# One core, attention and two mixing layers in one kernel: the first attention by head pairs, the second one later, small transfers on another queue, weight decoding spread evenly

## The chip, the core and the metric

The kernel runs on one core of a Trainium2 chip. The core has five engines that run their own instruction lists in order and meet only at semaphores: TensorE (PE in the profile, its weight loads as PEld) multiplies matrices, VectorE (DVE) and ScalarE (ACT) do elementwise work, GpSimd (POOL) sets memory here, and SyncE (SP) issues transfers. Any of SP, ACT and POOL can issue a transfer; it then stands in that engine's own list. The metric is the time of the whole program on the device, in microseconds. Half a per cent of it is 3.8 us.

## What is computed

Eight batches of 8 heads, 576 tokens and 64 channels a head. Three steps follow one another; the output is float32.

```python
kv = einsum('bhsd,bhse->bhde', k, v);  out = einsum('bhsd,bhde->bhse', q, kv)
x  = out / sqrt(mean(out*out, -1) + 1e-6) * g_norm          # linear attention, then (b, s, 512)
gate = sigmoid(sum_k conv_w[k] * x shifted by k)            # causal convolution, 5 taps
x  = gate * (x @ w_val) @ w_out
theta = x @ w_theta;  zr, zi = x*cos(theta), x*sin(theta)
u  = x + w_tok_r @ zr + w_tok_i @ zi                        # mixes tokens
out = u + relu(u @ w_ch)
```

The weights arrive as 64-bit floats. The kernel turns them into float32 by bit operations ("decoding"), and keeps each of them, and each operand of a large product, as a high part and a low part, so that one product is three matmuls.

## The kernel before

Channels lie on the 128 partitions as four blocks (`NM = 4`), tokens run along the free dimension in two halves of 288. The program has a start, a loop over the batches i = 0 to 7, and a last phase.

**Attention of one batch.** `load_kv` and `load_q` (lines 151 to 169) load keys and values (`kv`, four tiles, one for each pair of heads) and queries (`q`, two tiles) on SP's queue; a GpSimd memset goes ahead of each `kv` tile. `key_value` (171) multiplies keys by values into one PSUM tile `kvp`, which ACT copies to `kvs`. `attention` (187) is a generator in three pieces. The first two make a half of the tokens each: for both groups of pairs, 8 matmuls into `o`, the squares `sq` on ACT (204), and `x` = `o` times the norm's gain on ACT (205). The third piece sums the squares on PE (`ss`, 212), and DVE takes 1/sqrt in 12 small operations (219 to 225, the result is `y`, 128x72). For b >= 2 (`SPREAD`) `y` then goes to DRAM as `rd` and comes back spread over the partitions as `yb` (228 to 233), by transfers on SP's queue; for b = 0 and 1 PE spreads it by small matmuls.

**Normalizing.** `normalize` (237) multiplies `x` by `yb` on DVE (246 or 257) in two halves, and splits each into `xh` (ACT) and `xl` (DVE, line 69).

**First product and gate.** `conv` (261) makes the gate `acc` of one channel block: one multiplication on ACT, four multiply-adds on DVE (265), the sigmoid on ACT. `value` (278) makes for each block m 24 matmuls `v`, then DVE multiplies the gate by them (288) and the result is split into `gh` and `gl`. `first` (294) multiplies by `w_out` into `y` (lines 274 to 276 again), ACT copies to `yo`, SP stores it to DRAM as `yd`. In the trace the name `y` on PE is this product, and `y` on DVE is the 1/sqrt.

**The loop.** Batch i runs `value(i)`, and between its blocks `key_value(i+2)` (at m = 1, followed by the loads of `kv` for i+3) and the two halves of `attention(i+2)`; then `normalize(i+1)`, `first(i)` with the third piece of `attention(i+2)` in it, and the first two gates of i+1. Behind that stands the decoding of later weights: chunks `wt` of w_theta (`todo`) and `tk` of the token matrices (`toks`), each some four DVE passes of 128x512 (94 to 98); a decoded `tk` goes back to DRAM as `td`. `RATE = (1, 3)` asks for one `wt` and three `tk` in a batch, and batch 6 takes all that is left. These chunks have the lowest priority: the scheduler places them wherever the order of the program leaves an engine free by its own reckoning. `issue_after(x)` keeps what is under it behind x.

**The start.** `START` (31) is the order of the loads on SP's queue (v: chunks of w_val, o: of w_out, k: key and value tiles, q: queries, c: the taps and the gain; 0 to 3 belong to batch 0, 4 to 7 to batch 1). Then come `key_value(0)`, three chunks of w_val, the taps, `attention(0)`, `normalize(0)`, `key_value(1)`, `attention(1)`, the first gates, and the last chunk of w_val.

**Around i = 7.** The attention's memory is given back, `load_y(0)` loads the result of batch 0 (`f`) on SP's queue, DVE transposes it (`fT`, 321), it goes through DRAM (`sd`, `yt`), two chunks of w_ch are fetched on POOL's queue and decoded. Behind batch 7 the last phase begins: `theta` (`tht`, `th`), sines, and the token matrices `tok` read back from `td` and split into `wkh` and `wkl`, with which the products `u` start. From there on PE has the work of eight batches before it.

Of the kernel before, what the change touches and what calls it, by code (L numbers as in the profile page):

```python
# [8 lines left out]
F32 = mybir.dt.float32  # L9
# [21 lines left out]
START = "v0 k0 k1 v1 k2 k3 v2 q0 q1 q2 q3 c0 v3 o0 k4 k5 k6 k7 o1 q4 q5 q6 q7 o2 o3"  # L31
WVFIRST = 3
SPREAD = 2
EARLY = 2
RATE = (1, 3)
# [8 lines left out]
def attention_moe_holo_kernel(ctx, tc, kvm, kvt, qt, gn, w_val, conv_w, w_out, w_th, w_tok, w_ch, outT):  # L44
# [126 lines left out]
    def key_value(b, kv):  # L171

        ps = one_bank(f"kvp{b}")
        for g in range(2):
# [9 lines left out]
        kvs_of[b] = pa.tile([P, NP, D], F32, tag="kvs", bufs=2, name=f"kvs{b}")  # L184
        nc.scalar.activation(kvs_of[b], ps[:, 0:NP * D].rearrange("p (a e) -> p a e", e=D), AF.Copy)

    def attention(b, q):

        kv = kvs_of.pop(b)
# [3 lines left out]
        for h in range(2):  # L193
            sl = slice(h * HS, (h + 1) * HS)
            for g in range(2):
                o = two_banks(f"o{b}_{h}_{g}")
                for e in range(2):
                    for j in range(2):
                        rows = slice(j * D, (j + 1) * D)
                        mm = nc.tensor.matmul(o[e * D:(e + 1) * D, j, :], kv[rows, 2 * g + e, :], q[g][rows, e, sl],  # L200
                                              start=True, stop=True, tile_position=(j * D, e * D))
                ch = slice(2 * g, 2 * g + 2)
                sq[h, g] = px.tile([P, 2, HS], F32, tag="sq", bufs=4, name=f"sq{b}_{h}_{g}")
                nc.scalar.activation(sq[h, g], o, AF.Square, scale=0.125)
                nc.scalar.activation(x[:, ch, PAD + h * HS:PAD + (h + 1) * HS], o, AF.Copy, scale=gsb)
            yield x
# [19 lines left out]
        if b >= SPREAD:  # L226

            nc.sync.dma_start(out=rdram[b], in_=y)
            yb = px.tile([P, NM, S], F32, tag="yb", bufs=1, name=f"yb{b}")
            src = rdram[b].rearrange("(k r) x -> k (r x)", k=NM)  # L230
            for i in range(2):
                rows = src[:, i * S:(i + 1) * S].unsqueeze(0).to_broadcast([D, NM, S])
                nc.sync.dma_start(out=yb[i * D:(i + 1) * D], in_=rows)
# [35 lines left out]
    def product(ps, w, m, xh, xl, t0, chunks=range(4)):  # L269
        tsl = slice(t0, t0 + HS)  # L270
        wh, wl = w
        for k in chunks:
# [3 lines left out]
            nc.tensor.matmul(ps, wh[:, m, ks], xl[:, k, tsl], start=False, stop=(k == 3))  # L276

    def value(b, x, xh, xl, sg, between):
        gh = pa.tile([P, NM, S], F32R, tag="gh", bufs=1, name=f"gh{b}")
        gl = pa.tile([P, NM, S], F32R, tag="gl", bufs=1, name=f"gl{b}")  # L280
        for m in range(NM):
            between(m)
            g = sg[m]
            ps = two_banks(f"v{b}_{m}")
            for h in range(2):
                product(ps[:, h], wv, m, xh, xl, h * HS)
# [323 lines left out]
```

## Time and profile before

| | us |
|---|---|
| median of 3 runs | 752.65 (750.66 to 753.38) |
| the profiled execution | 753.31 |
| its span, first to last instruction | 751.5 |
| outside the span | 1.8 |
| PE busy | 709.7 |
| DVE busy | 523.9 |
| ACT busy | 335.9 |
| POOL busy | 20.7 |
| mean granted TensorE clock, share of full speed | 0.986 |

The profile is of one execution. The view of busy time by stretches gives for each stretch its length, then for each engine the busy time and the count of instructions, then the granted TensorE clock, the busy share of the transfer engines and GB/s. The views of waits name the waiting instruction, what it waited for, the total, how often, and the longest. In the timeline a row has the start, the busy time, the engine and line, the operation with its output and inputs, and in brackets the idle time before it with what ended it. A busy time of a group of "x2" or more runs from the first start to the last end.

### The profile page before, as it was taken

The numbers are of one execution on the slowest core, as the hardware profiler recorded it, in microseconds if no ns is written. First come the engines' busy times: TensorE is split into PE (matmuls) and PEld (weight loads), VectorE is DVE, ScalarE is ACT, GpSimd is POOL, SyncE is SP. The second block draws the span as 40 slices with busy tenths as digits, with TensorE's granted clock in tenths as the row PEclk, the third lists the DMA queues.
The fourth block names the chain that finished last, engine by engine and source line by source line (L and its number), as shares of the span: only waits on it lengthen the run. The fifth ranks groups of instructions, "written<-read, shape, count | busy, mean of one in ns | idle before, by whom it ended". The sixth has DMA issues, their size and how long they took to land.

```text
span 751.5 us, 14674 instructions
## 1 busy us (share of the span) xinstructions
PE 709.7 (94%) x6000; PEld 669.9 (89%) x6000; DVE 523.9 (70%) x930; ACT 335.9 (45%) x560; POOL 20.7 (3%) x72
## 2 busy tenths in 40 slices
PE   1679999999989999889999999999999999999998
PEld 1568999798987999879899899999999998998998
DVE  6389969798879999588983872853853835836504
ACT  2366565637464645376541640621622514514301
POOL 4000000000000000000000000000000000000000
PEclk9779999999999999999999999999999999999999
DMA  9948794979896358534345034163051270160101
GB/s 256 285 140 243 209 229 141 229 228 237 219 238 189 108 136 246 190 102 122 111 138 157 9 119 113 32 174 90 17 164 59 69 179 35 64 175 1 64 1 64
DMA packets 77059, 104.88 MB, mean 140 GB/s; under 512 B 11712, under 2 KB 42560, under 8 KB 76992
## 3 DMA queue, kind: packets, MB, share of 16 engines
q1 hardware_dynamic: 76416, 101.85, 48.5%
q0 software_dynamic: 576, 2.10, 0.9%
q8 instruction: 47, 0.77, 0.4%
q14 instruction: 20, 0.16, 0.1%
HBM read 72.73 MB, written 31.19 MB: 138 GB/s over the span
## 4 chain that ended last, share of the span: by engine, by line
PE 60%; DVE 24%; DMA 8%; ACT 4%; issue 3%; SPq 1%; POOL 0%; DVEq 0%; ACTq 0%; POOLq 0%
PE u L513 10%; PE u L511 10%; PE u L512 10%; DVE acc L265 10%; PE c L276 5%; PE c L274 5%; PE c L275 5%; DMA yb<-rd 4%; PE th L459 3%; PE th L457 3%; PE th L458 3%; DMA kv<-in_kvm_dram 2%; DVE x L246 2%; DVE xl L69 2%; DVE acc L288 2%
## 5 line engine op out<-in xcount | busy, mean ns | idle before, releaser
L516 DVE TENSOR_TENSOR f<-u,f 128x288 f32<-128x288 f32 x64 | 26.5, 455 | 129.8 <-PE u L513 129.8
L265 DVE SCALAR_TENSOR_TENSOR acc<-x,cw,acc 128x576 f32<-128x576 f32 x128 | 100.8, 817 | 1.3 <-ACT acc L263 1.3
L68 ACT ACTIVATE uh<-f 128x288 fp32r<-128x288 f32 x64 | 26.2, 444 | 152.4 <-DVE f L516 152.3
L274 PE MATMUL y<-gh,woh 128*128 128x288 f32 x256 | 77.8, 304 | 7.8 <-DVE acc L288 5.4
L274 PE MATMUL v<-xh,wvh 128*128 128x288 f32 x256 | 77.6, 303 | 0.7 <-DVE acc L288 0.7
L276 PE MATMUL v<-xl,wvh 128*128 128x288 f32 x256 | 76.5, 299 | 0.0
L276 PE MATMUL y<-gl,woh 128*128 128x288 f32 x256 | 75.8, 298 | 0.5 <-DVE gl L69 0.5
L275 PE MATMUL y<-gh,wol 128*128 128x288 f32 x256 | 76.0, 297 | 0.0
L275 PE MATMUL v<-xh,wvl 128*128 128x288 f32 x256 | 76.0, 297 | 0.0
L274 PE MATMUL c<-uh,wch 128*128 128x288 f32 x256 | 75.4, 295 | 0.0
L276 PE MATMUL c<-ul,wch 128*128 128x288 f32 x256 | 75.4, 295 | 0.0
L275 PE MATMUL c<-uh,wcl 128*128 128x288 f32 x256 | 75.4, 294 | 0.0
L274 PEld LDWEIGHTS y<-gh,woh 128*128 128x128 f32 x256 | 48.8, 191 | 11.9 <-DVE acc L288 6.1
L274 PEld LDWEIGHTS v<-xh,wvh 128*128 128x128 f32 x256 | 48.7, 190 | 4.6 <-issue 1.7
L459 PE MATMUL th<-wth,yl 128*128 128x512 f32 x128 | 50.3, 393 | 0.0
L458 PE MATMUL th<-wtl,yh 128*128 128x512 f32 x128 | 50.1, 391 | 0.0
L457 PE MATMUL th<-wth,yh 128*128 128x512 f32 x128 | 50.0, 391 | 0.0
L276 PEld LDWEIGHTS y<-gl,woh 128*128 128x128 f32 x256 | 48.4, 190 | 1.2 <-DVE gl L69 1.2
L276 PEld LDWEIGHTS v<-xl,wvh 128*128 128x128 f32 x256 | 48.6, 190 | 0.3 <-issue 0.2
L275 PEld LDWEIGHTS y<-gh,wol 128*128 128x128 f32 x256 | 48.8, 191 | 0.0
L275 PEld LDWEIGHTS v<-xh,wvl 128*128 128x128 f32 x256 | 48.7, 190 | 0.0
L275 PEld LDWEIGHTS c<-uh,wcl 128*128 128x128 f32 x256 | 48.0, 188 | 0.3
(188 smaller groups left out, 1946.0 us busy)
## 6 DMA issues: line engine op xcount, KB each, us to landing
kv<-in_kvm_dram SPq DMA_DIRECT2D x32, 512.0 KB, 8.6
q<-in_qt_dram SPq DMA_DIRECT2D x32, 288.0 KB, 8.9
yd<-yo SPq DMA_DIRECT2D x32, 288.0 KB, 2.4
f<-yd SPq DMA_DIRECT2D x32, 288.0 KB, 3.7
out_dram<-f SPq DMA_DIRECT2D x64, 144.0 KB, 1.8
sd<-fT SPq DMA_DIRECT2D x64, 128.0 KB, 2.5
yt<-sd SPq DMA_DIRECT2D x8, 1024.0 KB, 5.6
yb<-rd SPq DMA_DIRECT2D x12, 576.0 KB, 8.0
```

The source lines that it names most:

```text
L68: one = nc.scalar.activation(h, src, AF.Copy)
L265: nc.vector.scalar_tensor_tensor(a, x[:, m, k:k + S], cw[:, m * 5 + k:m * 5 + k + 1], a, ALU.mult, ALU.add)
L274: nc.tensor.matmul(ps, wh[:, m, ks], xh[:, k, tsl], start=(k == 0), stop=False)
L275: nc.tensor.matmul(ps, wl[:, m, ks], xh[:, k, tsl], start=False, stop=False)
L276: nc.tensor.matmul(ps, wh[:, m, ks], xl[:, k, tsl], start=False, stop=(k == 3))
L457: nc.tensor.matmul(ps, yh[:, k, :], wth[0][:, k, :], start=(k == 0), stop=False)
L458: nc.tensor.matmul(ps, yh[:, k, :], wth[1][:, k, :], start=False, stop=False)
L459: nc.tensor.matmul(ps, yl[:, k, :], wth[0][:, k, :], start=False, stop=(k == 3))
L511: nc.tensor.matmul(ps[:, :HS], zh[:, ms], wkh[:, j, sl], start=(i == 0), stop=False)
L512: nc.tensor.matmul(ps[:, :HS], zh[:, ms], wkl[:, j, sl], start=False, stop=False)
L513: nc.tensor.matmul(ps[:, :HS], zl[:, ms], wkh[:, j, sl], start=False, stop=(i == 8))
L516: nc.vector.tensor_tensor(f[:, m, sl], ps[:, :HS], f[:, m, sl], ALU.add)
```

## The change

- The first attention goes by groups of pairs of heads (both token halves of group 0, then of group 1), its `kvs` is copied group by group, and its `x` is written by DVE (`tensor_scalar`) and no longer by ACT. `START` has the queries of group 0 ahead of the third key tile, one chunk of w_val ahead of all, and the others behind the first batch; the gain is loaded on ACT's queue.
- Only one chunk of w_val is decoded ahead of the first attention, the taps behind it, and the other three chunks between the first gates.
- `key_value(1)` and `attention(1)` move from the start into `value(0)`, and the loads of batch 2 and `key_value(2)`, `attention(2)` behind them.
- `normalize(i+1)` is put behind DVE's `gl` of the last block of `value(i)` (`gs[2]` is the list of the four, `gs[2][-1]` the last), and the decoding of w_out behind that of the second block.
- `rd` and `yb` are issued by GpSimd.
- The third piece of the attention goes 12 matmuls earlier in `first`.
- `RATE` is (1, 2) in every batch from 1 to 6, and batch 6 takes no remainder.

```diff
-START = "v0 k0 k1 v1 k2 k3 v2 q0 q1 q2 q3 c0 v3 o0 k4 k5 k6 k7 o1 q4 q5 q6 q7 o2 o3"
-WVFIRST = 3
+START = "v0 k0 k1 q0 q1 k2 k3 q2 q3 v1 c0 v2 v3 k4 k5 k6 k7 o0 q4 q5 q6 q7 o1 o2 o3"
...
-RATE = (1, 3)
+RATE = (1, 2)
...
     def key_value(b, kv):
...
+        kvs_of[b] = pa.tile([P, NP, D], F32, tag="kvs", bufs=2, name=f"kvs{b}")
...
-        kvs_of[b] = pa.tile([P, NP, D], F32, tag="kvs", bufs=2, name=f"kvs{b}")
-        nc.scalar.activation(kvs_of[b], ps[:, 0:NP * D].rearrange("p (a e) -> p a e", e=D), AF.Copy)
...
-    def attention(b, q):
...
-        kv = kvs_of.pop(b)
+            if b == 0 or g == 1:
+                gs = slice(2 * g if b == 0 else 0, 2 * g + 2)
+                nc.scalar.activation(kvs_of[b][:, gs, :], ps[:, 0:NP * D].rearrange("p (a e) -> p a e", e=D)[:, gs], AF.Copy)
...
+    def attention(b, qs):
...
+        kv, q = kvs_of.pop(b), qs.pop(b)
...
-        for h in range(2):
+        for n in range(4):
...
+            g, h = divmod(n, 2) if b == 0 else (n % 2, n // 2)
...
-            for g in range(2):
-                o = two_banks(f"o{b}_{h}_{g}")
-                for e in range(2):
-                    for j in range(2):
-                        rows = slice(j * D, (j + 1) * D)
-                        mm = nc.tensor.matmul(o[e * D:(e + 1) * D, j, :], kv[rows, 2 * g + e, :], q[g][rows, e, sl],
-                                              start=True, stop=True, tile_position=(j * D, e * D))
-                ch = slice(2 * g, 2 * g + 2)
-                sq[h, g] = px.tile([P, 2, HS], F32, tag="sq", bufs=4, name=f"sq{b}_{h}_{g}")
-                nc.scalar.activation(sq[h, g], o, AF.Square, scale=0.125)
-                nc.scalar.activation(x[:, ch, PAD + h * HS:PAD + (h + 1) * HS], o, AF.Copy, scale=gsb)
-            yield x
+            o = two_banks(f"o{b}_{h}_{g}")
+            for e in range(2):
+                for j in range(2):
+                    rows = slice(j * D, (j + 1) * D)
+                    nc.tensor.matmul(o[e * D:(e + 1) * D, j, :], kv[rows, 2 * g + e, :], q[g][rows, e, sl],
+                                     start=True, stop=True, tile_position=(j * D, e * D))
+            xo = x[:, 2 * g:2 * g + 2, PAD + h * HS:PAD + (h + 1) * HS]
+            sq[h, g] = px.tile([P, 2, HS], F32, tag="sq", bufs=4, name=f"sq{b}_{h}_{g}")
+            nc.scalar.activation(sq[h, g], o, AF.Square, scale=0.125)
+            if b == 0:
+                nc.vector.tensor_scalar(xo, o, gsb, None, ALU.mult)
+            else:
+                nc.scalar.activation(xo, o, AF.Copy, scale=gsb)
+            if n % 2:
+                yield x
...
         sums = one_bank(f"ss{b}")[:, :TB]
...
         if b >= SPREAD:
...
-            nc.sync.dma_start(out=rdram[b], in_=y)
+            nc.gpsimd.dma_start(out=rdram[b], in_=y)
...
-                nc.sync.dma_start(out=yb[i * D:(i + 1) * D], in_=rows)
+                nc.gpsimd.dma_start(out=yb[i * D:(i + 1) * D], in_=rows)
...
-            nc.tensor.matmul(ps, wh[:, m, ks], xl[:, k, tsl], start=False, stop=(k == 3))
+            done = nc.tensor.matmul(ps, wh[:, m, ks], xl[:, k, tsl], start=False, stop=(k == 3))
+        return done
...
     def value(b, x, xh, xl, sg, between):
...
+        lasts, done = [], None
...
-            between(m)
+            between(m, done)
...
-                product(ps[:, h], wv, m, xh, xl, h * HS)
+                done = product(ps[:, h], wv, m, xh, xl, h * HS)
...
-            parts(gh[:, m, :], gl[:, m, :], g)
+            lasts.append(parts(gh[:, m, :], gl[:, m, :], g)[0])
...
-        return gh, gl
+        return gh, gl, lasts
...
     def first(b, gh, gl, between):
...
         part(0, range(3))
         part(1, range(3))
+        between()
...
-        between()
         part(2, range(4))
...
+    nc.scalar.dma_start(out=gsb[0:D], in_=gn)
+    nc.scalar.dma_start(out=gsb[D:P], in_=gn)
...
-            nc.sync.dma_start(out=gsb[0:D], in_=gn)
-            nc.sync.dma_start(out=gsb[D:P], in_=gn)
...
     key_value(0, kvs.pop(0))
-    for k in range(WVFIRST):
-        weight_chunk(px, wv, w_val, k, "wv", raw=raw[f"v{k}"])
+    weight_chunk(px, wv, w_val, 0, "wv", raw=raw["v0"])
+    *_, xy = attention(0, qs)
+    *_, (xs, last) = normalize(0, *xy)
...
-    *_, xy = attention(0, qs.pop(0))
-    *_, (xs, last) = normalize(0, *xy)
-    key_value(1, kvs.pop(1))
-    *_, xy = attention(1, qs.pop(1))
-    sg = [conv(0, m, xs[0]) for m in range(EARLY)]
-    with tc.issue_after(last.ins):
-        for n in range(WVFIRST, 4):
+    sg = []
+    for n in range(1, NM):
+        with tc.issue_after(last.ins):
...
-    kvs[2], qs[2] = load_kv(2), load_q(2)
+        if n <= EARLY:
+            sg.append(conv(0, n - 1, xs[0]))
...
-            ahead = attention(i + 2, qs.pop(i + 2))
...
-        def between(m):
...
-            if two and m == 1:
+            ahead = attention(i + 2, qs)
...
+        def between(m, done):
...
+            if i == 0 and m == 2:
+                with tc.issue_after(done.ins):
+                    key_value(1, kvs.pop(1))
+            if two and i and m == 1:
...
-                next(ahead)
...
+                next(ahead if i else second)
...
+        second = attention(1, qs) if i == 0 else None
...
+        if i == 0:
+            *_, xy = second
+            kvs[2], qs[2] = load_kv(2), load_q(2)
+            key_value(2, kvs.pop(2))
+            kvs[3] = load_kv(3)
+            next(ahead)
...
-            *_, (nxs, last) = normalize(i + 1, *xy)
+            with tc.issue_after(gs[2][-1].ins):
+                *_, (nxs, last) = normalize(i + 1, *xy)
...
-            for k in range(4):
-                weight_chunk(px, wo, w_out, k, "wo", raw=raw[f"o{k}"])
+            with tc.issue_after(gs[2][1].ins):
+                for k in range(4):
+                    weight_chunk(px, wo, w_out, k, "wo", raw=raw[f"o{k}"])
...
-        first(i, *gs, lambda: got.append(next(ahead) if two else None))
+        first(i, *gs[:2], lambda: got.append(next(ahead) if two else None))
...
-                for _ in range(RATE[0] if i < 6 else 8):
+                for _ in range(RATE[0]):
...
-                for _ in range(RATE[1] if i < 6 else 11):
+                for _ in range(RATE[1]):
...
```

The next rows are DVE's list in the program before, at the end of `value(1)`: `x_740` is the `x` of batch 2 and `yb_992` its 1/sqrt, `v_2`, `v_3`, `gl` belong to batch 1.

```order
L288 TENSOR_TENSOR acc_2_1095<-v_2_1196,acc_2_1095 128x576
L69 TENSOR_TENSOR gl_1066<-acc_2_1095,gh_1065 128x576
L246 TENSOR_TENSOR x_740<-x_740,yb_992 128x4x288 x2
L94 TENSOR_SCALAR dst_wt_1481<-raw_wt_1479 128x512
L288 TENSOR_TENSOR acc_3_1189<-v_3_1242,acc_3_1189 128x576
L95 SCALAR_TENSOR_TENSOR dst_wt_1481<-raw_wt_1479,dst_wt_1481 128x512
L69 TENSOR_TENSOR xl_1293<-x_740,xh_1292 128x4x288
L69 TENSOR_TENSOR gl_1066<-acc_3_1189,gh_1065 128x576
L69 TENSOR_TENSOR xl_1293<-x_740,xh_1292 128x4x288
```

The same place in the changed program, where the `x` of batch 2 is `x_769`.

```order
L296 TENSOR_TENSOR acc_2_1096<-v_2_1197,acc_2_1096 128x576
L68 TENSOR_TENSOR gl_1067<-acc_2_1096,gh_1066 128x576
L296 TENSOR_TENSOR acc_3_1190<-v_3_1243,acc_3_1190 128x576
L68 TENSOR_TENSOR gl_1067<-acc_3_1190,gh_1066 128x576
L252 TENSOR_TENSOR x_769<-x_769,yb_975 128x4x288 x2
L93 TENSOR_SCALAR dst_wt_1482<-raw_wt_1480 128x512
L68 TENSOR_TENSOR xl_1294<-x_769,xh_1293 128x4x288 x2
```

The multiplication by `yb` stood ahead of the multiplication by `v_3` and of the last `gl`; it now stands behind both.

DVE's list from the first normalization on, before: `x_282` is the `x` of batch 0, `acc_0` and `acc_1` are its first gates.

```order
L257 TENSOR_TENSOR x_282<-yb_0_0_367,x_282 128x2x288
L257 TENSOR_TENSOR x_282<-yb_0_1_377,x_282 128x2x288
L257 TENSOR_TENSOR x_282<-yb_1_0_389,x_282 128x2x288
L69 TENSOR_TENSOR xl_366<-x_282,xh_365 128x4x288
L257 TENSOR_TENSOR x_282<-yb_1_1_399,x_282 128x2x288
L265 SCALAR_TENSOR_TENSOR acc_0_537<-x_282,cw,acc_0_537 128x576
L265 SCALAR_TENSOR_TENSOR acc_1_544<-x_282,cw,acc_1_544 128x576
L69 TENSOR_TENSOR xl_366<-x_282,xh_365 128x4x288
L265 SCALAR_TENSOR_TENSOR acc_0_537<-x_282,cw,acc_0_537 128x576
L265 SCALAR_TENSOR_TENSOR acc_1_544<-x_282,cw,acc_1_544 128x576
```

And changed, with `x_260` for batch 0; `dst_wv_396` is the second chunk of w_val.

```order
L263 TENSOR_TENSOR x_260<-yb_1_0_367,x_260 128x2x288
L68 TENSOR_TENSOR xl_344<-x_260,xh_343 128x4x288
L263 TENSOR_TENSOR x_260<-yb_1_1_377,x_260 128x2x288
L93 TENSOR_SCALAR dst_wv_396<-raw_wv_170 128x512
L271 SCALAR_TENSOR_TENSOR acc_0_404<-x_260,cw,acc_0_404 128x576
L94 SCALAR_TENSOR_TENSOR dst_wv_396<-raw_wv_170,dst_wv_396 128x512
L68 TENSOR_TENSOR xl_344<-x_260,xh_343 128x4x288
L95 SCALAR_TENSOR_TENSOR dst_wv_396<-raw_wv_170,dst_wv_396 128x512
L271 SCALAR_TENSOR_TENSOR acc_0_404<-x_260,cw,acc_0_404 128x576
L97 SCALAR_TENSOR_TENSOR dst_wv_396<-raw_wv_170,dst_wv_396 128x512
```

The chunks of w_val that had been decoded before this place now stand between the gates and the splits of `x`.

SP's list at the end of batch 6, before: `f_3518` is the load of batch 0 for the last phase, `td` the store of a decoded chunk of the token matrices, `yd_76` the results of batch 6.

```order
L440 DMA td<-dst_tk_2844 128x512
L440 DMA td<-dst_tk_2853 128x64
L330 DMA f_3518<-yd_70 128x576 x2
L305 DMA yd_76<-yo_0_3432 128x576
L305 DMA yd_76<-yo_1_3441 128x576
L330 DMA f_3518<-yd_70 128x576 x2
L346 DMA ft_3547<-yd_70 128x4x64
L305 DMA yd_76<-yo_2_3469 128x576
L346 DMA ft_3547<-yd_71 128x4x64
L330 DMA f_4027<-yd_71 128x576
```

And changed, where the load is `f_3519` and the last, short chunk is `dst_tk_3508`. That chunk's last pass stands on DVE behind the multiplication by `v_1` of batch 7.

```order
L313 DMA yd_76<-yo_0_3424 128x576
L313 DMA yd_76<-yo_1_3433 128x576
L313 DMA yd_76<-yo_2_3461 128x576
L313 DMA yd_76<-yo_3_3489 128x576
L458 DMA td<-dst_tk_3508 128x64
L338 DMA f_3519<-yd_70 128x576 x4
L354 DMA ft_3548<-yd_70 128x4x64
L354 DMA ft_3548<-yd_71 128x4x64
L338 DMA f_4028<-yd_71 128x576 x2
L333 DMA sd_86<-fT_0_3524 32x8x128 x4
```

The loads of `f` stood between the stores of batch 6 in part; they now stand behind all of these and behind the store of the last chunk.

## The prediction

> **What bounds the kernel now.** I read the span by stretches first, cut where the start, each batch of the loop and the last phase begin. Columns: length, then busy time and count for PE, its weight loads, DVE, ACT and POOL, the granted clock, the transfer engines' share, GB/s.
>
> ```profile
> 0.00:48.50 48.50, 22.51 (x384) 18.68 (x384) 28.52 (x51) 20.37 (x33) 10.90 (x42) 0.88 0.94 258
> 48.50:89.60 41.10, 40.99 (x467) 36.67 (x466) 38.17 (x74) 24.75 (x40) 1.51 (x5) 0.94 0.74 199
> 89.60:121.70 32.10, 32.10 (x370) 30.05 (x370) 25.96 (x44) 18.18 (x28) 1.18 (x5) 1.00 0.73 187
> 121.70:155.90 34.20, 32.68 (x370) 30.09 (x370) 29.58 (x50) 19.48 (x30) 1.19 (x5) 1.00 0.85 220
> 155.90:189.10 33.20, 32.42 (x371) 29.97 (x370) 29.98 (x51) 19.44 (x31) 1.80 (x5) 1.00 0.85 224
> 189.10:224.20 35.10, 32.39 (x370) 30.04 (x370) 27.70 (x49) 17.96 (x29) 1.45 (x5) 1.00 0.89 222
> 224.20:258.90 34.70, 32.69 (x370) 29.95 (x369) 34.35 (x61) 21.37 (x34) 0.39 (x1) 1.00 0.52 159
> 258.90:286.10 27.20, 25.96 (x194) 25.49 (x193) 25.66 (x44) 14.18 (x23) 0.00 (x0) 1.00 0.51 146
> 286.10:315.20 29.10, 27.18 (x194) 26.95 (x193) 22.48 (x33) 10.75 (x17) 1.22 (x2) 0.94 0.68 211
> 315.20:334.00 18.80, 16.36 (x78) 13.20 (x76) 13.83 (x22) 12.32 (x19) 0.00 (x0) 1.00 0.44 131
> 334.00:751.50 417.50, 414.38 (x2853) 398.80 (x2853) 247.67 (x463) 157.10 (x282) 1.06 (x2) 1.00 0.30 89
> ```
>
> From 334 us on PE is busy for 414.4 of 417.5 us, and the change does not reach there. All that can be won lies ahead of it. In the first row PE works for 22.5 of 48.5 us: 26 us are idle. The third row is a batch with nothing in its way, 32.1 us and all of it PE. The next four, with the same 370 matmuls, sum to 34.2 + 33.2 + 35.1 + 34.7 = 137.2 us: 8.8 above four times 32.1. In the fifth batch DVE is busy for 34.35 of 34.70 us, so there DVE is the bound.
>
> The waits say what stops PE and DVE.
>
> ```profile
> PE y L274 <- DVE acc L288: 5.4, 3, 2.5
> PE ss L212 <- ACT sq L204: 4.7, 3, 3.3
> PE yb L254 <- DVE y L225: 3.1, 1, 3.1
> DVE x L246 <- DMA yb<-rd: 6.2, 3, 3.4
> ```
>
> The second and third are the start's 1/sqrt. The first and the last belong together, as batch 4 (from 189.1) shows in the timeline of its 1/sqrt:
>
> ```profile
> 195.15 0.24 DVE L225 SCALAR_TENSOR_TENSOR y<-t,y 128x72 f32<-128x72 f32 x1
> 195.41 0.33 SPq L228 DMA_DIRECT2D rd<-y  x1
> 197.19 1.25 SPq L233 DMA_DIRECT2D yb<-rd  x2
> 209.07 2.63 DVE L246 TENSOR_TENSOR x<-x,yb 128x1152 f32<-128x1152 f32 x2 [3.40 <-DMA yb<-rd]
> 211.62 0.75 DVE L288 TENSOR_TENSOR acc<-v,acc 128x576 f32<-128x576 f32 x1
> ```
>
> The 1/sqrt is ready at 195.39, `yb` is there at 209.07: a flight of 13.7 us. DVE stands still for 3.40 us and works 2.63 more before it may multiply by `v_3` at 211.62, and PE waits for that product (up to 2.5 us) to begin `y`.
>
> **The loop.** The order of DVE's list takes `x` by `yb` out of the way: behind `v_3` and the last `gl`. What does a batch then hold on DVE? The counts are from its list, sixteen gates' multiply-adds, four multiplications, four `gl`, two `x`, two `xl`, three chunks, and the small ones; the durations from these rows:
>
> ```profile
> L265 DVE SCALAR_TENSOR_TENSOR acc<-x,cw,acc 128x576 f32<-128x576 f32 x68 | 54.0, 816 | 0.9 <-ACT acc L263 0.9
> L69 DVE TENSOR_TENSOR gl<-acc,gh 128x576 fp32r<-128x576 f32 x16 | 12.1, 757 | 3.7 <-ACT gh L68 3.7
> L69 DVE TENSOR_TENSOR xl<-x,xh 128x1152 fp32r<-128x1152 f32 x8 | 10.7, 1353 | 4.5 <-ACT xh L68 4.5
> L95 DVE SCALAR_TENSOR_TENSOR dst_tk<-raw_tk,dst_tk 128x512 int32<-128x512 int32 x9 | 6.2, 692 | 0.1
> L94 DVE TENSOR_SCALAR dst_tk<-raw_tk 128x512 int32<-128x512 int32 x8 | 3.4, 425 | 0.0
> L225 DVE SCALAR_TENSOR_TENSOR y<-t,y 128x72 f32<-128x72 f32 x13 | 3.1, 235 | 0.0
> 41.66 4.46 DVE L265 SCALAR_TENSOR_TENSOR acc<-x,cw,acc 128x576 f32<-128x576 f32 x6
> ```
>
> 16 x 0.82 + 8 x 0.76 + 4 x 1.35 + 3 x (0.43 + 3 x 0.69) + 0.69 + 12 x 0.23 = 13.1 + 6.1 + 5.4 + 7.5 + 0.7 + 2.8 = 35.6 us. Six multiply-adds in a row take 4.46, not 4.90: each begins 0.09 before the last one's end. The 53 instructions so overlap by 4.6 us, which leaves 31.0. That is under 32.1, but not by much, and it is now the same in batches 2 to 5, where DVE had 27.7 to 34.35 (mean 30.4). So neither engine is over the PE floor, and both are near it. Lists that run in order and hand work to each other do not both run at 97%; I add 0.5 us a batch, which is a little under what the best of the four, the 33.2 us batch with DVE at 30.0, shows (1.1, of which a part is the wait for `yb`). Four batches at 32.6 are 130.4: **-6.8 us**. Bounds: -8.8 (all four at the floor) and -2 (all but the 34.70 batch and the 3.40 wait stay as they are). Batch 6 goes from 27.2 towards PE's 25.96, as its decoding falls from four chunks to two: **-0.9** (0 to -1.2).
>
> This supposes that `yb` still comes in time on GpSimd's queue. Its transfers and one load that GpSimd issued already:
>
> ```profile
> yb<-rd SPq DMA_DIRECT2D x12, 576.0 KB, 8.0
> raw_wc<-in_w_ch_dram POOLq DMA_DIRECT2D x4, 512.0 KB, 5.8
> raw_wt<-in_w_th_dram SPq DMA_DIRECT2D x4, 512.0 KB, 5.2
> ```
>
> At the same size GpSimd's load landed in 5.8 us and SP's in 5.2, in different stages. So I price the queue at +0.6 a transfer, twice in a row (`rd`, then `yb`): a flight of 15 us instead of 13.7, with 0 to +6 as bounds (+6: one of the two takes as long again as the 5.8; a shorter flight than 13.7 gains nothing, since the slot is later). What it has: DVE was ready for it at 209.07 - 3.40 = 205.67, so 10.3 us after 195.39; the new slot is later by the 24 matmuls of `v_3` (24 of 370 of 32.1 us are 2.1) and by the multiplication and `gl` (1.5), and the 1/sqrt is earlier by the 12 matmuls that its sums are moved over (1.0) and by the gates that no longer wait for the decoding (three of 0.73, estimated). 10.3 + 2.1 + 1.5 + 1.0 + 2.2 = 17 us. It holds with 2 us to spare. The Trainium skill ("SBUF — State Buffer", section "SBUF: two separate sides") speaks against this part: GpSimd, it says, writes the descriptors of its transfers itself, and cannot while DVE runs an operation in a two-port mode. By the page that would touch the 128x512 `tensor_scalar` of a chunk and not the multiply-adds, so three times 0.43 us a batch at most; whether the blocking goes further no row here shows, apart from the 5.8. On GpSimd the memsets of the next keys are queued behind the `yb` issue, which waits for `rd`; their tiles are wanted a batch later, so that costs nothing. SP's list loses the issue that waited for `y`, and the key loads behind it go out sooner, into the same time as `yb`: this is what the +6 has to cover.
>
> **The start.** The chain before, and its ends:
>
> ```profile
> 19.38 1.86 PE L182 MATMUL kvp<-kv 128*64 128x64 f32 x30 [2.11 <-DMA kv<-in_kvm_dram]
> 28.02 0.78 ACT L205 ACTIVATE x<-o,gsb 128x576 f32<-128x576 f32 x1
> 28.96 0.23 DVE L219 TENSOR_SCALAR ss<-ss 128x72 f32<-128x72 f32 x1 [2.71 <-PE ss L212]
> 33.99 0.76 DVE L257 TENSOR_TENSOR x<-yb,x 128x576 f32<-128x576 f32 x1 [2.17 <-PE yb L254]
> 48.53 0.61 PE L274 MATMUL v<-xh,wvh 128*128 128x288 f32 x1
> 81.34 0.69 DVE L69 TENSOR_TENSOR wol<-dst_wo,woh 128x512 fp32r<-128x512 f32 x1
> ```
>
> By the order of the loads, until the last key tile of batch 0 is in with the queries that are in flight beside it, 4.52 MB come (three chunks of w_val of 512 KB, four key tiles of 576, two query loads of 288), now 4.06 (one chunk, four tiles, four query loads): 0.46 MB at the 258 GB/s of the first stretch are 1.8 us. Behind it stood four squares and four copies on ACT, 6 us; now two squares (the first pair's are done) while DVE copies `x` beside them, so 3.9 us less. The sum of squares ends 5.7 us earlier, at 23.3. `v` no longer waits for batch 1's keys and attention and starts near 32.7 rather than 48.5. But the work has only changed places. DVE's list from there to the last chunk of w_out holds 20 multiply-adds, seven chunks (2.5 us each, and 0.69 for the low part), eight `x`, four `xl`, four multiplications, four `gl` and 28 small ones, 103 instructions: 16.4 + 17.5 + 4.8 + 6.1 + 5.4 + 6.1 + 6.4 = 62.7 us, less overlaps of 0.09 for all but the first 12 small ones, 8: 55 us, to 78.3 without any wait. The keys of batch 1 are used only inside `value(0)`, so those of batch 2, which take over their tiles, land near 60, and `x` of batch 1 is scaled near 72: I estimate 6.5 us of such waits, about what PE lost in this stretch to two of the three waits quoted (3.3 and 3.1). The last chunk is decoded at 84.8, not at 81.34 + 0.69 = 82.0, then the 24 matmuls of the last block (2.1 us, and what stands before them in PE's list, 4 in all) follow, and batch 1 begins at 88.8, against 89.6: **-0.8**, with -7 (no wait at all) and +4 (five more) as bounds. The copies of `x` on DVE are 4 x 0.76 = 3 us of this.
>
> **The end of the loop.** On SP the loads of `f` stand behind the store of the last small chunk, whose last pass waits on DVE behind `v_1` of batch 7. Before:
>
> ```profile
> 275.49 0.85 SPq L330 DMA_DIRECT2D f<-yd  x2
> 288.63 2.37 DVE L321 STREAM_TRANSPOSE fT<-f 128x1024 f32<-128x1024 f32 x2
> 300.00:303.00 3.00, 1.08 (x8) 0.85 (x7) 2.98 (x5) 1.20 (x2) 0.00 (x0) 1.00 0.90 332
> 303.00:306.40 3.40, 3.40 (x17) 3.40 (x16) 2.42 (x4) 1.02 (x3) 0.00 (x0) 0.50 0.48 181
> ```
>
> The loads began 10.6 us ahead of batch 7 (286.1) and the transposes 2.5 us behind its start. Now the loads go out about 10 us into it (after 16 multiply-adds), the transposes come at 17 to 19. Batch 7's own gates then run without the transposes in between, and its matmuls end at about 26 us instead of 29.1. But the rest waits: transposes 2.4, five splits, the stores, the fetch of w_ch at 5.8 us, two chunks of 3.2 us on DVE. I find the first `u` 45.8 us behind the start of batch 7, where it was 44.4, that is +1.5, with PE idle for some 5 us on the way. The last two rows show the price of an idle stretch: PE was idle for 1.9 us of three and then ran 3.4 us at half clock. One such stretch is +1.7 of lost work, of which I take +1: **+2.5**, between 0 and +6. The Trainium skill ("TensorE: Matmul & The Clock Gate", Part 1) has the clock fall to half after an idle window of some 3.4 us; here 1.9 us were enough, so the rows decide, and by the page alone the half-clock stretch would be left out of the term, which would be +1.5.
>
> **The sum.** -6.8 - 0.9 - 0.8 + 2.5 = -6.0 against the profiled 753.3, so 747.3; the profiled execution lies 0.7 above the median of 752.65, so on that scale 746.6: **747**.
>
> **Rivals.** *Late `yb` (slower).* GpSimd's two transfers take longer against the key loads than supposed. The 2 us to spare and the 0.5 us that I gave each batch are used up at a flight of 17.5; from there each us is lost in all four batches. At 20 us that is +10, 757; at 21, 761. For it: two transfers in a row, and a batch's transfers already fill 0.85 of the engines. Against it: the 5.8 us row. *Given back (same).* The loop wins its 7.7, but the start's waits are longer (+3 instead of -0.8) and the end costs 4.5: 753.3 - 7.7 + 3 + 4.5 = 753.1, or 752.4 by the median. For it: both stretches are paced by loads and DVE, not PE. *The start pays.* DVE's waits there are mostly hidden by the decoding: batch 1 begins at 84, -5.6 instead of -0.8, so 742; against it stands the late loading of batch 2's keys. *The loop stays.* The overlaps fail, with DVE at 33 us a batch: 33.4 each, -3.6 instead of -6.8, so 750, within the same bound.
>
> **Chances.** Forecast (743.5 to 749.5) 0.45, start pays 0.12, given back 0.16, loop stays 0.11, late `yb` 0.16. Half a per cent is 3.8 us (748.9 and 756.4), about what a measurement of this kernel can tell from no change. Faster: 0.44 of the forecast and 0.12, 0.56. Same: 0.01, 0.16 and 0.11 less a little that falls out on the slow side, 0.27. Slower: 0.17. The range leaves out most of the late `yb` (0.13) and the best of the start (0.05): 740 to 756.
>
> **What would show it.** Right: no wait of `x` for `yb` ahead of the multiplication by `v_3`, batches 2 to 5 at 32 to 33 us with DVE at 30 to 32 busy, `ss` of batch 0 on DVE near 23.3, `v` near 33, batch 1 near 89, `f`'s loads some 10 us into batch 7, first `u` some 46 us behind its start. Wrong: a wait of `x` or of PE's `v` for `yb` in every batch; batch 1 well before 86 or after 91; an end that costs over 6 us.

## The result and the profile after

The changed kernel is slower: 759.95 us median (758.71 to 761.68, 4 runs) against 752.0 (750.66 to 753.38, 4 runs), a ratio of 1.0101 with a 95% interval of 1.0072 to 1.0130. The profiled execution took 758.71 us with a span of 756.9. Its span is 5.4 us longer than the one of before; the medians lie 8.0 apart, since the profile of before is of an execution 1.3 us above its median and this one is 1.2 below. The 5.4 can be located, the rest is scatter between executions.

The view by stretches, cut as before: the start, batches 1 to 7, the time from theta to the first `u`, the first products, the rest.

```profile
0.00:89.60 89.60, 65.99 (x849) 54.71 (x850) 68.53 (x128) 42.76 (x68) 11.84 (x47) 0.92 0.80 226
89.60:121.70 32.10, 32.10 (x370) 30.05 (x370) 24.64 (x41) 17.66 (x27) 3.20 (x8) 1.00 0.78 209
121.70:153.80 32.10, 32.10 (x370) 30.05 (x370) 29.48 (x50) 18.84 (x30) 2.98 (x8) 1.00 0.87 241
153.80:187.50 33.70, 32.34 (x370) 29.89 (x369) 30.71 (x54) 19.90 (x31) 3.25 (x8) 1.00 0.82 236
187.50:221.80 34.30, 32.58 (x370) 29.99 (x369) 31.38 (x54) 19.92 (x31) 3.24 (x8) 1.00 0.83 240
221.80:255.90 34.10, 32.55 (x371) 30.03 (x370) 33.14 (x58) 21.17 (x33) 1.90 (x4) 1.00 0.44 131
255.90:281.70 25.80, 25.69 (x194) 25.46 (x194) 24.78 (x40) 12.90 (x19) 1.79 (x3) 1.00 0.41 114
281.70:307.10 25.40, 25.40 (x194) 25.40 (x193) 19.63 (x29) 10.05 (x16) 0.57 (x1) 1.00 0.53 140
307.10:334.20 27.10, 14.20 (x63) 11.02 (x61) 12.88 (x21) 11.84 (x19) 0.56 (x1) 0.86 0.59 188
334.20:377.00 42.80, 42.62 (x265) 40.31 (x266) 36.61 (x65) 25.19 (x46) 1.07 (x2) 0.93 0.44 130
```

Batch 1 begins at 89.6 in both: the start is worth nothing. Batches 2 to 5 sum to 134.2 us, 3.0 less than the 137.2 of before, with batch 2 at the floor of 32.1 and the others 1.6 to 2.2 above it. Batch 6 is 1.4 shorter. So batch 7 begins at 281.7, 4.4 us earlier than before, and its matmuls are done at 307.1, 8.2 earlier. Then, where 15.2 us passed before the first `u`, 27.1 pass: PE is busy for 14.2 of them. From the start of batch 7 to the first `u` it is 52.5 us; it was 44.4. The end gives back 8.2 us, and the first products run 1.5 longer (their clock is 0.93). -3.0 - 1.4 + 8.2 + 1.5 is the 5.4, to 0.1.

The waits in the changed kernel, the first of PE, the others of DVE:

```profile
PE u L529 <- ACT wkh L67: 12.3, 1, 12.3
DVE dst_wc L93 <- DMA st<-fTt: 13.0, 1, 13.0
DVE dst_wt L93 <- DMA td<-dst_tk: 5.6, 3, 2.0
```

No row says that `x` waited for `yb`: it is gone, as forecast. Two new ones stand there. One is a wait of 13.0 us for the buffer of a decoded chunk of w_ch; the timeline of DVE shows what is behind it in the list:

```profile
299.20 2.36 DVE L329 STREAM_TRANSPOSE fT<-f 128x1024 f32<-128x1024 f32 x2
302.06 0.76 DVE L329 STREAM_TRANSPOSE fTt<-ft 128x256 f32<-128x256 f32 x2
302.74 0.65 DVE L68 TENSOR_TENSOR tl<-ft,th 128x512 fp32r<-128x512 f32 x1
316.37 0.43 DVE L93 TENSOR_SCALAR dst_wc<-raw_wc 128x512 int32<-128x512 int32 x1 [12.98 <-DMA st<-fTt]
...
324.47 0.68 DVE L479 TENSOR_SCALAR frt<-tht 128x512 f32<-128x512 f32 x1
```

`frt`, the first step from theta to the sines and so to `u`, had its input soon after 310 and ran at 324.47. The chunk's buffer is the one in which the transposed tails `fTt` lie until their store `st` has landed. SP's list gives the time of that store:

```profile
291.74 0.32 SPq L458 DMA_DIRECT2D td<-dst_tk  x1
292.11 1.85 SPq L338 DMA_DIRECT2D f<-yd  x4
300.46 4.27 SPq L333 DMA_DIRECT2D sd<-fT  x8
304.83 1.40 SPq L333 DMA_DIRECT2D st<-fTt  x3
306.84 0.39 SPq L347 DMA_DIRECT2D yt<-sd  x1
307.27 0.50 SPq L333 DMA_DIRECT2D st<-fTt  x1
```

The last `st` is issued at 307.27, just behind the 1 MB load of `yt`, and lands some 9 us later. Its slowness is not new. The view of the tile `st` (its stores and the loads of `ytt` from it) gives the landing times, in the kernel before and in the changed one:

```profile
DMA to landing us min/median/max: 1.7/2.7/8.9
DMA to landing us min/median/max: 1.7/2.6/9.0
```

The slowest is the same last store in both. What is new is when it goes out: 25.6 us into batch 7, where it was 11.7. In the kernel before it had landed 20.6 us into batch 7, while DVE was still at the gates, and the decoding of w_ch began at 21.5 without a wait for it.

The other new wait is at the end of batches 2, 3 and 4:

```profile
174.61 2.62 DVE L252 TENSOR_TENSOR x<-x,yb 128x1152 f32<-128x1152 f32 x2
179.25 0.43 DVE L93 TENSOR_SCALAR dst_wt<-raw_wt 128x512 int32<-128x512 int32 x1 [2.03 <-DMA td<-dst_tk]
179.60 2.62 DVE L68 TENSOR_TENSOR xl<-x,xh 128x1152 fp32r<-128x1152 f32 x2
```

A chunk of w_theta is to be decoded between `x` and `xl`; its buffer is still being stored as `td`, and DVE stands for 2 us with the next batch's gates behind it.

### The profile page after: what moved, and what is told of

It reads as the page before. It is cut to its first block, busy times and chain, and to the rows that moved or that the text cites. A ratio compares the mean times of both kernels' runs of the same rounds, so it can differ in the third digit from the quotient of the medians.

```text
span 756.9 us, 14673 instructions
## 1 busy us (share of the span) xinstructions
PE 712.2 (94%) x6000; PEld 669.9 (89%) x6000; DVE 526.1 (70%) x934; ACT 333.4 (44%) x557; POOL 30.4 (4%) x90
## 4 chain that ended last, share of the span: by engine, by line
PE 69%; DVE 17%; DMA 8%; ACT 3%; issue 2%; SPq 1%; DVEq 0%; ACTq 0%
PE u L530 10%; PE u L529 10%; PE u L531 10%; DVE acc L271 7%; PE c L282 4%; PE c L281 4%; PE c L280 4%; PE th L477 3%; PE th L475 3%; PE th L476 3%; DMA td<-dst_tk 3%; DMA kv<-in_kvm_dram 2%; PE y L280 2%; PE v L280 2%; PE y L282 2%
```

## The experiments

Two theories stood ahead of them. **Ours**: the end costs 8 us since the last, short chunk of the token matrices falls into batch 7 and everything of `f` comes behind it; the loop loses 6 more to the decode buffers. **The rival**: GpSimd's queue, or the even decoding itself, is what costs. Times are medians, with the ratio to the kernel before on the same chip; "span" is that of a profiled execution, "the end" the time from the start of batch 7 to the first `u` (44.4 before, 52.5 after).

**The changed kernel again** (as a base on the chip on which three of the kernels below ran: the decoding tied to `gl`, the chunk earlier with `yb` on SP, and the old start).

> The changed kernel itself, on the chip of the three others, as their base: 758 to 762 us, the first u 52 to 53 us behind the start of batch 7, batches 3 to 5 at 33.5 to 34.3.

Measured: 761.4 us, 1.0105 (1.0070 to 1.0141). The end 52.1, batches 3 to 5 at 33.4, 34.6 and 33.9.

**The short chunk one batch earlier.**

```diff
-                for _ in range(RATE[1]):
+                for _ in range(RATE[1] + (i == 5)):
```

> The changed kernel with one thing different: the last, short chunk of the token matrices is taken in batch 5 and not in batch 6, so that its store no longer stands ahead of the loads of f, and DVE's list has the transposes of f between the gates of batch 7 again. Theory (the end of the loop pays: f is loaded 10 us late, and all that hangs on it collides): the first u comes 44 to 46 us behind the start of batch 7 instead of 52.5, DVE's wait of 13.0 us for a store is gone, and the time falls by 8 to 10 us from the changed kernel's 760, to 750 to 752. Rival (the loss is the transfers on GpSimd's queue): no change, 759 to 761. Rival (the even decoding itself costs): no gain, or 1 us more, since batch 5 decodes one more small chunk.

Measured: 751.5 us, 0.9972 (0.9943 to 1.0000). The end 42.3 us, 2 us better than expected. In the timeline of DVE the transposes of `f` come 1.9 us behind the start of batch 7 (284.5), and the decode of w_ch starts without a wait:

```profile
286.42 2.36 DVE L329 STREAM_TRANSPOSE fT<-f 128x1024 f32<-128x1024 f32 x2
305.41 0.42 DVE L93 TENSOR_SCALAR dst_wc<-raw_wc 128x512 int32<-128x512 int32 x1
316.38 0.68 DVE L479 TENSOR_SCALAR frt<-tht 128x512 f32<-128x512 f32 x1
```

The place of one small chunk is worth some 10 us at the end (from 52.1 to 52.5 down to 42.3). The last store `st` still takes 8.7 us here; it goes out earlier, and DVE has other work until it lands. Batch 6 paid 2.1 of it back (28.0 for 25.8).

**The store of that chunk on GpSimd.** The arguments of `decode` are left out here:

```diff
-                        nc.sync.dma_start(out=tokdram[:, sl], in_=decode(...))
+                        (nc.gpsimd if j == 10 else nc.sync).dma_start(out=tokdram[:, sl], in_=decode(...))
```

> The changed kernel with the store of the last, short chunk issued by GpSimd. SP's list is free of it and the loads of f go out some 12 us earlier; but the order on DVE stays, with the transposes behind all gates of batch 7. Theory (both the late loads and the late transposes count): the first u at 48 to 51 us behind the start of batch 7, 756 to 758. Rival (only SP's order counts): like the kernel with the chunk taken earlier, 750 to 752.

Measured: 759.66 us, 1.0084 (1.0056 to 1.0113). The end 52.8: nothing won, both expectations missed. With the store gone from SP's list, the loads of `f` still go out 10 us into batch 7 (which began at 280.8). The timeline of DVE and SP shows what they waited for:

```profile
290.63 0.22 DVE L97 SCALAR_TENSOR_TENSOR dst_tk<-raw_tk,dst_tk 128x64 f32<-128x64 f32 x1
...
290.88 1.77 SPq L338 DMA_DIRECT2D f<-yd  x4
```

The loads start 0.03 us behind the end of the chunk's last pass, and the view of waits puts their wait down to it:

```profile
SPq L338 <- DVE dst_tk L97: 8.7, 1, 8.7
```

So it was not the place in SP's queue that made them late but the decode itself. Why they wait for it is read from the program and not shown by a view: the loads use no data of the chunk, but `f` lies in memory that the attention's pool gave back, and this pass is the last one to read the chunk as it was fetched (`raw_tk`). The store of the decoded chunk went out only at 291.1, behind the loads, so they did not wait for that one.

**No w_ch ahead of the last phase.**

```diff
-CHFIRST = 2
+CHFIRST = 0
```

> The changed kernel with the order of the end unchanged (loads of f late, transposes behind the gates of batch 7), but no chunk of w_ch fetched and decoded ahead of the last phase: all four are decoded during the first products u. In the changed kernel the decode of w_ch waits 13.0 us for the store that frees its buffer, and the first sines' operands stand behind it on DVE. Theory A (that wait in DVE's list is the last link): the operands follow theta at once, the first u comes 44 to 47 us behind the start of batch 7 instead of 52.5, and 6 to 8 us are won, 752 to 754. Theory B (the transfers themselves are the last link: the 1 MB of transposed f and the tails land only some 35 us behind the start of batch 7 whatever DVE does): without 1 MB of w_ch in the same stretch they land 3 us earlier, the first u at 48 to 50, 756 to 757.

Measured: 761.85 us, 1.0118 (1.0075 to 1.0160). The end 42.5, with the loads of `f` and the transposes as late as in the changed kernel. The last `st` did land in 5.9 us instead of 9.0, the 3 us of theory B, but the end came 10 us earlier: the transfers were not the last link, DVE's list was (theory A, and more than it asked for). The time was missed by both theories: the four chunks then hold up the last products instead, in the waits of PE behind 340 us:

```profile
PE c L280 <- ACT wch L67: 6.5, 3, 3.5
PE c L281 <- DVE wcl L68: 1.5, 2, 0.7
```

From the first `c` to the end it is 390.4 us, where the changed kernel has 379.9.

**The decoding tied to `gl` and not to `x`.**

```diff
-            with tc.high_priority(offset=-LATER), tc.issue_after(last.ins):
+            with tc.high_priority(offset=-LATER), tc.issue_after(gs[2][2].ins):
```

> The changed kernel with one name different: the decoding of the later weights is kept behind the gl of the third block of the batch and no longer behind the multiplication of x by yb. Theory (the change moved that multiplication behind the last gl and the decoding with it, since the decoding is tied to it, so that the last chunk of batch 6 fell into batch 7): SP's list has the loads of f among the stores of batch 6 again, the first u at 42 to 45 behind batch 7, and 7 to 9 us are won, 750 to 753, with rates, buffers and queues as changed; batches 3 to 5 stay at 32.5 to 34. Rival (the small chunk is late for want of room on DVE): the end stays at 50 or more, 757 or more.

Measured: 754.43 us, 0.9998 (0.9970 to 1.0026). The end 42.3: without this tie the last store of a chunk goes out in batch 6 again, 13.7 us into it, so it was not for want of room on DVE that it was late. The decoding has always been kept behind `last`, the multiplication by `yb`; that one moved behind the last `gl`, and the decoding went with it, past the end of the batch. The loop came out worse than expected, 32.8, 34.6, 35.6 and 36.7 us, with DVE waiting 7.9 us for decode buffers (four waits), and with it the time missed the expected 750 to 753.

**The moved normalization alone**, on the kernel before (`value` also returns its list of `gl` here).

```diff
-            *_, (nxs, last) = normalize(i + 1, *xy)
+            with tc.issue_after(gs[2][-1].ins):
+                *_, (nxs, last) = normalize(i + 1, *xy)
```

> The kernel before with one part of the change alone: the normalization of the next batch behind the last gl of the batch. Everything else is old, the start, SP's queue for yb, the rates. Theory (x by yb ahead of the multiplication by v_3 cost the loop most of its 8.8 us): DVE's wait for yb is gone, batches 2 to 4 at 32.1 to 32.8, batch 5 stays near 34.5 as DVE is full there, 4 to 5 us less than before, 747 to 749. Rival (the loss in the loop is the amount of decoding): within 1 us of before.

Measured: 758.8 us, 1.0064 (1.0036 to 1.0092). The loop did as the theory says and more: 32.1, 32.1, 33.4 and 32.5 us, 7.2 less than before in the four (batch 6 is 1.8 longer). But the time missed both expectations, mainly since the end is 52.2, with the same wait:

```profile
DVE dst_wc L94 <- DMA st<-fTt: 13.2, 1, 13.2
```

The rates are the old ones here, and still the last chunk slipped into batch 7 (its store goes out 9.1 us into it). So this one edit is enough both for the gain in the loop and for the loss at the end.

**Three buffers for decoded chunks.** A part of one line, the count of buffers of the tile `dst`:

```diff
-bufs=(1 if tag else 2) if pool is px else 1
+bufs=(1 if tag else 3) if pool is px else 1
```

> The changed kernel with three buffers instead of two for decoded chunks. In batches 3 to 5 of the changed kernel DVE waited 2.0 us each for the store of an older chunk before it began a new one, and these batches took 33.8 to 34.3 us where batches 1 and 2 took 32.1. Theory (that wait delays the decoding into the gates, and ACT's list behind it): the three batches fall to 32.1 to 32.8, 4 to 6 us less, 754 to 756. Rival (three chunks a batch are simply too much work on DVE and ACT next to the gates): the wait goes, the batches stay at 33.5 or more, and the time stays within 1.5 us of 760.

Measured: 754.67 us, 1.0016 (0.9986 to 1.0046). Batches 2 to 5 at 32.11 each, to the floor; the end stays at 52.2.

**`rd` and `yb` on SP again.**

> The changed kernel with rd and yb issued by SP again. Theory: yb was in time on either queue, since x by yb now stands behind the last gl; batches 1 to 6 change by less than 0.5 us each and the time stays within 2 us of 760. Rival (late yb on GpSimd, or GpSimd's queue in the way of others): 4 us or more are won back, 756 or less.

Measured: 754.43 us, 1.0011 (0.9984 to 1.0037): expected wrongly; the number is the rival's. Batches 3 to 5 fell to 32.2. But it is not a late `yb`: `x` waited for it on neither queue. The scheduler made another list, and the chunk of w_theta no longer stands between `x` and `xl`:

```profile
174.45 2.62 DVE L252 TENSOR_TENSOR x<-x,yb 128x1152 f32<-128x1152 f32 x2
177.17 2.63 DVE L68 TENSOR_TENSOR xl<-x,xh 128x1152 fp32r<-128x1152 f32 x2
```

With three buffers the same 32.1 come with `yb` on GpSimd; so the gain does not need SP's queue: what both runs take away is the wait for the buffer.

**The old rates in the changed kernel.**

```diff
-RATE = (1, 2)
+RATE = (1, 3)
```

(and the remainder in batch 6 as before.)

> The changed kernel with the old rates of decoding: one chunk of w_theta and three of the token matrices a batch, and the remainder in batch 6. The order on SP and DVE at the end is then the old one, with the loads of f among the stores of batch 6 and the transposes among the gates of batch 7. Theory (the even decoding is what spoils the end): the first u at 42 to 45 us behind the start of batch 7, as with the small chunk taken earlier; batches 3 to 5 at 33 to 35, since a fourth chunk comes on DVE; 749 to 752. Rival (the end is spoiled by other parts, the transfers on GpSimd or the moved normalization): the first u stays at 50 or more, 758 to 760.

Measured: 764.87 us, 1.0145 (1.0099 to 1.0192). The end 44.4, as expected: with three chunks a batch none is left for batch 6. But batches 3 to 5 took 41.2, 38.2 and 37.6, and the time missed both expectations. DVE waited 15.1 us for decode buffers, up to 4.9 at a time, with PE behind it and a granted clock of 0.88, 0.91 and 0.95 in these batches. So the even rate has a part in the late end of the changed kernel, by leaving the short chunk to batch 6, but it saves more than that: batches 2 to 5 sum to 149.1 us without it and to 134.2 with it.

**Both mendings.** The short chunk in batch 5, three buffers.

> The changed kernel with both mendings: the short chunk taken in batch 5 and three buffers for decoded chunks. Theory (the two losses are apart): the sum of both gains, batches 2 to 5 at 32.1 to 32.6, the first u at 42 to 44 behind batch 7, span 743 to 744.5, 744 to 747 us. Rival (they are one loss seen twice): no better than the better of the two, 751.

Measured: 744.08 us, 0.9865 (0.9829 to 0.9900). Its stretches, batch 2, batch 5 and from batch 7 on:

```profile
124.60:156.70 32.10, 32.10 (x370) 30.05 (x370) 31.02 (x54) 19.61 (x31) 2.97 (x8) 1.00 0.85 242
...
220.90:253.00 32.10, 32.10 (x371) 30.05 (x370) 31.02 (x54) 21.24 (x33) 1.91 (x4) 1.00 0.46 141
...
278.80:305.90 27.10, 25.78 (x194) 25.52 (x193) 21.89 (x32) 9.99 (x16) 1.13 (x2) 1.00 0.71 213
305.90:321.10 15.20, 13.95 (x62) 11.13 (x60) 10.25 (x16) 10.60 (x17) 0.00 (x0) 1.00 0.41 123
```

DVE is busy for 31.02 us of every batch of 32.10, and PE does not lose a tenth. The two losses are apart, and their mendings add up: against the changed kernel's 1.0105 the ratio falls by 0.024, where the chunk alone gave 0.013 and the buffers alone 0.009.

**The chunk earlier and `yb` on SP**, two buffers.

> The changed kernel with the short chunk taken in batch 5 and rd and yb on SP again, two buffers for decoded chunks as changed. Theory (GpSimd's queue as such costs nothing; in the kernel with yb on SP the list of DVE came out without the wait for a store): as good as with three buffers, batches 2 to 4 at 32.1 to 32.3, batch 5 up to 33, the first u at 42 to 44, 743 to 747. Rival (the two changes of the list do not add up, since the short chunk moves the others): 748 to 752.

Measured: 745.37 us, 0.9894 (0.9859 to 0.9929). Batches 2 to 5 at 32.1 to 32.2, the end 43.0. It agrees.

**The old start with the mended loop.** The kernel before, with the moved normalization, the rate (1, 2), and both mendings.

> The kernel before with the moved normalization, the rates (1, 2) and the two mendings (short chunk in batch 5, three buffers for decoded chunks); the start, the place of the second attention, SP's queue for yb and the place of the sums stay old. Theory (the loop's part is the whole gain; new start, GpSimd's queue and the earlier sums are worth nothing): batches 2 to 5 at 32.1 to 32.6, the first u 42 to 45 behind batch 7, the start of batch 1 within 2 us of the kernel with both mendings, 743 to 747. Rival (the new start or the other queue carries part of it): 748 to 751.

Measured: 742.68 us, 0.9857 (0.9827 to 0.9888), span 741.4. Batch 1 begins at 90.9, with both mendings and the new start at 92.5. Batches 2 to 5 take 32.1, 32.2, 32.5 and 32.2 us, the end 42.3. The first attention by pairs, the later second one, the copies on DVE, GpSimd's queue and the earlier sums bring nothing that can be seen: in all runs batch 1 begins at 89.6 to 93.0 with the new start and at 89.6 to 92.3 with the old one. This is the version to keep: as fast as the other, with a handful of lines changed.

## Why the prediction was wrong

Forecast was a gain of 6.0 us of span; the span grew by 5.4. Of the 11.4 us between them, 7.2 are the end's (with its slower clock) and 3.8 the loop's; the start and batch 6 are right to within 1 us.

**The loop: right in its cause, wrong in a term.** The wait of `x` ahead of `v_3` was the loss, as far as the runs part the causes: the moved normalization alone wins 7.2 there, forecast 6.8, and no wait for `yb` is left, but the decoding tied to it moves with it. With that tie cut, the four batches take 139.6 us, 7.9 of them waits of PE behind a DVE that stands for decode buffers. The tally of DVE held too: 31.0 us forecast, 31.02 measured once nothing made DVE wait. The step that failed is "Lists that run in order and hand work to each other do not both run at 97%; I add 0.5 us a batch". Here they do: three buffers, and both mendings, leave batches of 32.1 us. What stood in its place is a named wait, the chunk's buffer behind the store of an older chunk, 2 us in three batches, with a DVE that has 1 us to spare. Measured -3.0. The number of buffers of the decode was in the code; I had priced the passes of a chunk and not what its first pass waits for.

**`yb` on GpSimd: right.** From the end of the 1/sqrt to the landing of `yb` the changed kernel took 11.3 to 15.6 us (15 forecast), and `x` was multiplied 16.1 to 17.2 us behind it in the batches up to 5 (17 forecast), so `yb` was always there. The loads landed in 8.0 us (median) on both queues, `rd` in 2.3 instead of 1.5. With `yb` on SP again the whole way took 10.2 to 12.2 us (9.9 to 13.7 in the kernel before); whether the blocking by DVE that the Trainium skill warns of ("SBUF — State Buffer", "SBUF: two separate sides") has a part in the difference, no run here shows. The rival that was to be slower for a late `yb` is refuted.

**Batch 6: right in kind**, -1.4 for -0.9, a little past its bound of -1.2.

**The start: right**, 0.0 for -0.8. The sum of squares came at 25.3, not 23.3, but `v` began at 32.1 (32.7), the last chunk of w_out ended at 85.3 (84.8), batch 1 began at 89.6 (88.8). The work had only changed places, as the list of DVE said; other runs of this start scatter by more than the forecast 0.8.

**The end: this decided it.** +2.5 was forecast, between 0 and +6; +8.2 was measured, and 1.5 more at half clock, where I had put 1. The loads of `f` (10.4 us into batch 7) and the transposes (17.5) came when forecast. The step that failed is "the fetch of w_ch at 5.8 us, two chunks of 3.2 us on DVE": it took the decode to begin when the fetch lands. The fetches, issued at 305.1 and 307.3, took 4.6 and 8.0 us, so they were there at 309.7 and 315.4; DVE was idle, but the decode began at 316.37 and its second chunk at 320.48. It begins when its buffer is free, and that was the tails' until their last store landed, 9.0 us after its issue. `frt`, behind the chunks in DVE's list, came 42.8 us into batch 7, and `u` at 52.5 instead of 45.8. With the buffer free the second chunk could have begun at 315.4, 5 us earlier; by this estimate the buffer is most of the 6.7 that were missed, and the second fetch (8.0 for 5.8) the rest. No run gave this decode a buffer of its own, so that share is not measured.

Both slow transfers could be seen in the trace of before: there too the last `st` took 8.9 us and the second fetch 7.9. The 5.8 was a median of four fetches, and DVE did not have to wait for that store, so the views of waits did not point at it. The fall of the end from 52.1 to 42.3, by nothing but the place of one small chunk, and to 42.5 with w_ch out of DVE's list, shows both links: the late chunk, and the decode of w_ch ahead of `frt`. The stretch of idle PE on the way, forecast at 5 us, came as 12.3 us in one piece.

The reason that I gave for the late loads was not the right one either. They came when forecast since the store, which I thought they waited for, stands behind the same pass on DVE; for the reason that was luck. I read it off SP's list, where the loads stand behind the store of the last chunk. With that store elsewhere they were as late: they wait for the chunk's last pass on DVE, most likely for the memory of the fetched chunk, over which `f` is laid.

## What to carry to other kernels

A list of instructions shows what stands behind what; it does not show for which buffer an instruction waits. For each instruction that is moved or now stands ahead of a chain, ask what its output's memory held before, and when that is released: by a read, or by a store that has yet to land. And price a transfer by what it took at that place in the trace, not by the median of its kind. Low-priority work that is tied to a point in the program goes where the point goes; look at its last piece, and at what begins when the memory is given back. Where a bundle loses, test its parts one by one: here one edit held a gain of 7 us and a loss of 8, and two more lines turned 1.0105 into 0.9865.

## What the runs showed of the hardware

In the kernel with both mendings PE and DVE ran for four batches in a row at 32.10 of 32.10 and 31.02 of 32.10 us busy, handing work to each other throughout: these two lists needed no margin for their hand-overs.

In the changed kernel, after the 12.3 us in which PE waited for its first `u` operand, the granted clock was 0.50 from 334.2 to 338.6 and 0.93 over the whole next 42.8 us, and that stretch took 1.5 us longer than the 41.3 of before. In the kernel with both mendings, which passes the same place in 15.2 us, the clock there is 1.00.

A store of 64 KB that went out just behind a 1 MB load on SP's queue took 7.4 to 9.7 us to land in every kernel that fetched w_ch beside it, and 5.9 without that fetch; the median of such stores is 1.8.
